# Window attention into a swish feed-forward layer: head-pair loads, coarser crossbar DMAs, and a refitted DMA model in the planner that orders the instructions

## The chip, the cores and the metric

The kernel runs on one core of a Trainium2 chip. The metric is device microseconds of one execution: a median over runs. "Span" is the time from the first to the last instruction in a profiled run, some 2 us less than the device time. Ratios and their intervals use fast runs alone; four of the medians below include one slow run each, that is, one over 1.5% above the fastest of its kernel.

## The reference

Four batches of 8 heads, 768 tokens, 64 channels. Each query sees the 128 keys up to its own and the first 4 keys ("sinks"). The attention output of 3072 tokens x 512 then passes through a feed-forward layer with 2048 hidden channels.

```python
keep   = is_sink | in_window                      # (768, 768)
a      = softmax(where(keep, q @ k.T / 8, -1e9))
x      = (a @ v).transpose(0, 2, 1, 3).reshape(3072, 512)
h      = x @ w_in                                 # 512 -> 2048
out    = (h * sigmoid(beta * h)) @ w_out          # 2048 -> 512
```

## The kernel before

The work is cut into eight half batches (384 tokens), each with four units (pairs of heads). For a unit, q and k are loaded in float32, cast to bfloat16, transposed, multiplied into scores; ScalarE takes the exponential; TensorE multiplies with v; VectorE normalises; the result is transposed into `xT`, the input of the feed-forward part. In half batches 0 to 2 TensorE does the transposes. From half batch 3 on the DMA does them ("crossbar" transposes, DMA_TRANSPOSE in the trace). SyncE issues all loads, stores and crossbar DMAs, one after the other.

The order is fixed before the kernel runs: while it is built, a planner gives every operation a start and an end by assumed durations, and sorts them. Each engine then gets its list and works through it in that order, waiting in line for what an entry needs:

```python
    def place(self, o, at):                       # the planner's clock
        o.at = at
        if o.dma:
            self.free[o.eng] = at + o.queue       # SyncE is taken for the issue
            self.dma_free = max(self.dma_free, at + 1100) + 1.15 * o.ns
            o.end = self.dma_free + 1000          # landed
        else:
            o.end = self.free[o.eng] = at + o.ns
...
    def emit(self, nc, block, sems):              # what each engine gets
        def run(eng, handle):
            for o in self.ops:                    # in the planned order
                if o.eng != eng:
                    continue
                for s, c in o.waits:
                    handle.wait_ge(sems[s], c)
                ins = o.fn(handle)
```

So the DMA engines are one pipe to the planner: each transfer takes 1.15 times its assumed duration, and lands 1 us later. The durations are formulas such as `524288 / 370` ns for a weight load. A planned landing decides at which place of an engine's list the cast of that load stands.

The two DMA issues that the change makes coarser:

```python
    def XT(hb, i, c):                             # q: three DMAs of 4 blocks, k: one of 12
        n, s0 = "qk"[i], 4 * hb % NT
        cs = [c] if i == 0 else list(range(NK))
        ...
            x16[n][hb % NX][:, cs[0]:cs[0] + len(cs), :, :]...), XNS * len(cs), ... queue=XQ)

    def XO(u):                                    # one DMA per unit (3 blocks)
        ...
            xT[:, hp, t0:t0 + HALF]...,
            onorm[on][:, :, :, :]...), XNS * 0.75, ... queue=XQ)
```

and the list of loads, by pairs in half batch 0 only:

```python
    def xl(hb):
        if hb >= XB:                              # XB = 3
            return [(hb, n, i) for n in "qkv" for i in range(NK)]
        if hb:                                    # 1 and 2: q and k whole, 768 KB each
            return [(hb, "q", None), (hb, "k", None)] + [(hb, "v", c) for c in range(NK)]
        return [(0, n, i) for i in range(4) for n in "qk"] + [(0, "v", c) for c in range(NK)]
```

The softmax here doesn't subtract the row's maximum and nothing guards it: scores larger than these inputs give would overflow.

## Time and profile before

| | kernel before |
|---|---|
| time, median of 3 runs | 235.44 us (235.38 to 237.55) |
| profiled span, mean granted clock | 232.9 us, 0.999 |
| first feed-forward matmul | 23.6 us |
| crossbar DMAs, their issue time on SyncE | 40, 59.7 us |
| the planner's own end | 231.4 us |

The table of stretches, SyncE's queue and the chain are shown in the prediction. One more line of before is wanted for later. It is the group of value matmuls (probabilities times v), with TensorE's idle time ahead of them in the last column:

```profile
L708 PE MATMUL P<-vaug,E 128*128 128x65 bf16 x352 | 19.0, 193 | 1.1 <-DVE vaug L453 0.7
```

TensorE waits 1.1 us in all for these 352 matmuls: the order gets to each of them when its inputs are ready.

### The profile page before, as it was taken

The page shows a single profiled execution, that of the slowest core. Times are in us where ns is not written, and L with a number is a line of the kernel's source. Part 1 is how long each engine was busy: PE and PEld are TensorE (multiplying, and loading weights), DVE is VectorE, ACT ScalarE, POOL GpSimd, SP SyncE. Part 2 cuts the span into 40 slices and gives each one's busy share as a digit, 9 for nine tenths or more (in the row PEclk, how much of TensorE's full clock was granted, in tenths as well). Part 3 has the DMA queues.
Part 4 walks back from the last instruction along what each step waited for, and adds up shares of the span by engine and source line. Part 5 has one row for each costly group of instructions (what it writes and reads, how often), then busy time and mean ns, then how long its engine had stood idle before and what let it go on. Part 6 is the DMA issues. An engine that isn't in the chain of part 4 may idle for free.

```text
span 232.9 us, 4577 instructions
## 1 busy us (share of the span) xinstructions
PE 218.9 (94%) x1756; PEld 122.0 (52%) x1756; DVE 136.8 (59%) x291; ACT 152.6 (66%) x276; POOL 72.5 (31%) x163
## 2 busy tenths in 40 slices
PE   7976999899999999998989999999999999999993
PEld 5554555456555555545446555554555555555541
DVE  3795689977764459527739657946553533633310
ACT  3958978578864889439974757776754655645431
POOL 6584943023450337108355104601740000000000
PEclk9999999999999999999999999999999999999999
DMA  6999999999669998694969999977412111011112
GB/s 182 244 335 245 331 363 389 352 235 228 145 155 237 241 272 162 144 176 72 182 133 232 147 227 222 174 170 169 155 34 65 45 45 45 4 45 45 45 48 90
DMA packets 94677, 39.76 MB, mean 171 GB/s; under 512 B 81328, under 2 KB 87488, under 8 KB 94656
## 3 DMA queue, kind: packets, MB, share of 16 engines
q1 hardware_dynamic: 94656, 39.47, 71.4%
q8 instruction: 14, 0.23, 0.4%
q14 instruction: 7, 0.06, 0.1%
HBM read 27.27 MB, written 6.29 MB: 144 GB/s over the span
## 4 chain that ended last, share of the span: by engine, by line
PE 69%; DMA 9%; DVE 8%; ACT 7%; SPq 4%; issue 1%; POOL 0%
PE P L775 34%; PE P L755 26%; DMA v_stage<-in_v_dram 5%; DMA wst<-in_moe_w_in_dram 4%; DVE g L762 3%; ACT E L645 3%; PE P L708 3%; PE P L637 3%; ACT t L760 2%; SPq L740 2%; SPq L512 2%; DVE vaug L453 2%; DVE onorm L714 1%; ACT qkT L448 1%; PE P L698 1%
## 5 line engine op out<-in xcount | busy, mean ns | idle before, releaser
L760 ACT ACTIVATE t<-P,hbeta 128x384 f32<-128x384 f32 x128 | 73.5, 591 | 43.4 <-PE P L755 39.7
L755 PE MATMUL P<-xT,w_in 128*128 128x384 bf16 x512 | 97.3, 326 | 0.9 <-DVE w_in L453 0.6
L775 PE MATMUL P<-w_out,g 128*128 128x512 bf16 x384 | 96.0, 379 | 2.1 <-DVE g L762 1.9
L762 DVE SCALAR_TENSOR_TENSOR g<-t,P 128x384 bf16<-128x384 f32 x128 | 69.2, 548 | 48.4 <-ACT t L760 46.4
L651 POOL TENSOR_SCALAR_AFFINE_SELECT E<-E 128x512 bf16<-128x512 bf16 (+1 forms) x112 | 54.7, 519 | 68.5 <-ACT E L645 67.9
L755 PEld LDWEIGHTS P<-xT,w_in 128*128 128x128 bf16 x512 | 48.0, 98 | 39.3 <-DVE w_in L453 1.4
L775 PEld LDWEIGHTS P<-w_out,g 128*128 128x128 bf16 x384 | 35.9, 98 | 38.3 <-DVE g L762 4.0
L645 ACT ACTIVATE E<-P 128x768 bf16<-128x768 f32 x64 | 45.5, 777 | 5.6 <-PE P L637 5.5
L448 ACT ACTIVATE osb<-P 128x512 f32<-128x512 f32 x19 | 11.4, 598 | 14.6 <-PE P L775 14.6
L708 PE MATMUL P<-vaug,E 128*128 128x65 bf16 x352 | 19.0, 193 | 1.1 <-DVE vaug L453 0.7
L708 PEld LDWEIGHTS P<-vaug,E 128*128 128x128 bf16 x352 | 16.5, 97 | 4.4 <-DVE vaug L453 0.9
L714 DVE TENSOR_TENSOR onorm<-P,rden 128x384 bf16<-128x384 f32 x32 | 17.7, 554 | 0.9 <-DMA xT<-onorm 0.2
L637 PE MATMUL P<-qkT 64*128 64x128 bf16 (+1 forms) x256 | 16.8, 239 | 1.5 <-ACT E L645 1.3
L453 DVE CAST q<-q_stage 128x512 bf16<-128x512 f32 (+1 forms) x19 | 10.1, 541 | 8.5 <-DMA q_stage<-in_q_dram 8.3
L637 PEld LDWEIGHTS P<-qkT 64*128 64x128 bf16 x256 | 8.7, 94 | 11.6 <-issue 4.5
L453 DVE CAST vaug<-v_stage 128x512 bf16<-128x512 f32 x19 | 9.0, 473 | 7.2 <-DMA v_stage<-in_v_dram 7.1
L698 PE MATMUL P<-vS,ES 128*128 128x130 bf16 x64 | 12.7, 220 | 0.0
L712 DVE RECIPROCAL rden<-P 128x6 f32<-128x6 f32 x32 | 6.1, 189 | 9.8 <-PE P L708 9.7
L672 ACT ACTIVATE ES<-P 128x128 bf16<-128x128 f32 (+1 forms) x32 | 11.1, 421 | 0.0
L448 ACT ACTIVATE xT<-P 128x384 bf16<-128x384 bf16 x11 | 5.4, 493 | 7.2 <-PE P L727 7.2
L453 DVE CAST k<-k_stage 128x512 bf16<-128x512 f32 (+1 forms) x15 | 6.9, 465 | 4.9 <-DMA k_stage<-in_k_dram 4.7
L954 PE MATMUL P<-ones 128*128 128x256 bf16 x47 | 8.5, 315 | 1.1 <-POOL ones L459 1.1
(50 smaller groups left out, 101.9 us busy)
## 6 DMA issues: line engine op xcount, KB each, us to landing
v_stage<-in_v_dram SPq DMA_DIRECT2D x24, 256.0 KB, 4.6
out_dram<-osb SPq DMA_DIRECT2D x24, 256.0 KB, 2.4
k_stage<-in_k_dram SPq DMA_DIRECT2D x15, 256.0 KB, 4.6
q_stage<-in_q_dram SPq DMA_DIRECT2D x15, 256.0 KB, 4.8
wst<-in_moe_w_in_dram SPq DMA_DIRECT2D x5, 512.0 KB, 8.6
wst<-in_moe_w_out_dram SPq DMA_DIRECT2D x4, 512.0 KB, 6.8
g<-in_moe_w_out_dram SPq DMA_DIRECT2D x4, 512.0 KB, 7.2
q_stage<-in_q_dram SPq DMA_DIRECT2D x2, 768.0 KB, 7.6
```

Of the source, the lines that this page charges most:

```text
L448: return lambda e: e.activation(dst, src, AF.Copy, bias=0.0, scale=scale)
L453: return lambda e: e.tensor_copy(dst, src)
L637: add("pe", lambda e, dst=dst, own=own, kc=kc, rows=rows, q0=q0, nq=nq: e.matmul(dst, tokens(own, 1, rows, kc, 1)[:, 0, :], tokens(u, 0, r ...
L645: add("act", lambda e, src=src, dst_=dst_: e.activation(dst_, src, AF.Exp, bias=0.0, scale=SCALE), act_ns(256 * n), w=[(k_, z, j) for k_ i ...
L651: add("gp", lambda e, d=d, sg=sg, at_=at_: e.affine_select(d, d, [[0, 2 * len(at_)], [sg, 128]], ALU.is_ge, 0.0, base=min(sg, 0), channel_ ...
L698: add("pe", lambda e, m=m, c0=c0: e.matmul(A[:, c0:c0 + 2 * (D + 1)], ES[z][:, m * 128:(m + 1) * 128], vS[b % 2][:, 2 * hp:2 * hp + 2, :]. ...
L708: e.matmul(A[:, c0:c0 + D + 1], E[z][:, i, hh, :], vaug[vz][:, kb % NK, 2 * hp + hh, :], start=a, stop=o, skip_group_check=True), 39,
L714: add("dve", lambda e: e.tensor_tensor(onorm[on][:, :, :, :].rearrange("p m h d -> p (m h) d"), av[:, :, 0:D], rden[on][:, :].unsqueeze(2) ...
L755: add("pe", lambda e, c=c: e.matmul(hp, w_in16[:, c, m * 128:(m + 1) * 128], xT[:, c, t0:t0 + HALF], start=(c == 0), stop=(c == 3)), mm_ns ...
L760: add("act", lambda e: e.activation(tt[ti][:, :], hp, AF.Tanh, bias=0.0, scale=hbeta[:, m:m + 1]), act_ns(HALF) + 93, r=["hbeta"], w=[("t" ...
L762: add("dve", lambda e: e.scalar_tensor_tensor(gt[T_ % NG][:, m, :], tt[ti][:, :], 1.0, hp, ALU.add, ALU.mult), dve_ns(HALF), r=[("t", ti)] ...
L775: add("pe", lambda e, m=m: e.matmul(P[:, bk, :], gt[T_ % NG][:, m, t * 128:(t + 1) * 128], w_out16[:, m, :], start=(m == 0), stop=(m == NM ...
```

## The change

It has three parts. q and k of half batch 1 are loaded by head pairs, eight DMAs of 192 KB in place of two of 768 KB, so that casts can begin earlier. The crossbar DMAs become fewer: one per tensor and half batch for q and k (q's three of 4 blocks become one of 12, as k has it already), and one per two units for the output. Third, the planner's DMA durations are set to rounded values near the spacings seen in traces, and the factor 1.15 on them goes. Line numbers fall by one to five; L453 of before is L452 of after.

```diff
-            self.dma_free = max(self.dma_free, at + 1100) + 1.15 * o.ns
+            self.dma_free = max(self.dma_free, at + 1100) + o.ns
@@ loads (v, and q and k from half batch 3 on)
-            ... [i], 262144 / 240
+            ... [i], 1110
@@ loads by pairs, whole loads
-            keys, ns = ([i], 196608 / 350) if i is not None else (range(4), 786432 / 350)
+            keys, ns = ([i], 680) if i is not None else (range(4), 2450)
@@ weights; stores
-        ... 524288 / 370, ...
+        ... 1390, ...
-            ... 262144 / 300, ...
+            ... 700, ...
@@ crossbar of q and k
-    def XT(hb, i, c):
-        cs = [c] if i == 0 else list(range(NK))
-            ... XNS * len(cs), ... queue=XQ)        # 700 each block row, 1300
+    def XT(hb, i):
+        cs = list(range(NK))
+            ... 1700, ... queue=1540)
@@ crossbar of the output
-            xT[:, hp, t0:t0 + HALF]..., onorm[on][...]..., XNS * 0.75, ... queue=XQ)
+            xT[:, u // 4, hp:hp + 2, :]..., onorm[:, on:on + 2, :, :]..., 1000, ... queue=1350)
@@ which half batches are loaded and cast by pairs
+    XB, PB = 3, 2
-        if hb:
+        if hb >= PB:
             return [(hb, "q", None), (hb, "k", None)] + [(hb, "v", c) for c in range(NK)]
-        return [(0, n, i) for i in range(4) for n in "qk"] + [(0, "v", c) for c in range(NK)]
+        return [(hb, n, i) for i in range(4) for n in "qk"] + [(hb, "v", c) for c in range(NK)]
```

(Cut: the layouts of `xT` and `onorm` that the wider output transpose needs, and the counts of casts that gate each step.)

More of the change, by code (lines that the diff above doesn't have):

```diff
@@ L348, in _program @@
     NSTG, NX, NV, NT, NE, NON, NG, NTT, NOS, NKS, NWS = 2, 2, 3, 8, 4, 4, 3, 3, 3, 4, 6
-    XB = 3
-    XQ, XNS = 1300, 700
+    XB, PB = 3, 2
     NK = NB // 2
@@ L359, in _program @@
     headm = sb("headm", (128, 2), BF16)
-    xT = sb("xT", (128, 4, NTOK), BF16)
+    xT = sb("xT", (128, NSB, 4, HALF), BF16)
     w_in16 = sb("w_in16", (128, 4, DF), BF16)
@@ L372, in _program @@
     vS = sb("vS", (128, H, D + 1), BF16, 2)
-    onorm = sb("onorm", (128, NK, 2, D), BF16, NON)
+    onorm = sb("onorm", (128, NON, NK * 2, D), BF16)
     rden = sb("rden", (128, 2 * NK), F32, NON)
@@ L502, in load @@
             src = v[b, :, t0 + i * 128:t0 + (i + 1) * 128, :].rearrange("h p d -> p h d")
-            dst, keys, ns = stg[n][z][:, i, :, :], [i], 262144 / 240
+            dst, keys, ns = stg[n][z][:, i, :, :], [i], 1110
         elif hb >= XB:
             src = {"q": q, "k": k}[n][b, :, t0 + i * 128:t0 + (i + 1) * 128, :].rearrange("h p d -> p h d")
-            dst, keys, ns = blocks(stg[n][z])[:, i, :, :], [i], 262144 / 240
+            dst, keys, ns = blocks(stg[n][z])[:, i, :, :], [i], 1110
         else:
@@ L521, in load_w @@
             src = w_out_src[:, 2 * (j - 8):2 * (j - 8) + 2, :]
-        add("sp", lambda e: e.dma_start(wst[j % NWS], src), 524288 / 370, w=[("wst", j % NWS)], dma=f"dw{j % NWS}")
+        add("sp", lambda e: e.dma_start(wst[j % NWS], src), 1390, w=[("wst", j % NWS)], dma=f"dw{j % NWS}")
     def cast_w(j):
@@ L538, in cast @@
             r, w = [("stg", n, z, i), ("vones", hb % NV)], [("v", hb % NV, i)]
-        elif hb == 0:
+        elif hb < PB:
             hs = slice(2 * i, 2 * i + 2)
@@ L549, in cast @@
             r, w = [("stg", n, z, j) for j in range(4)], [(n + "16", hb % NX, j, i) for j in range(4)]
-        if hb == 0 and n != "v":
+        if hb < PB and n != "v":
             ns = {"act": 413, "dve": 400}
@@ L597, in XT @@
             qkT_all[:, hb % (NT // 4), i, cs[0] * 512:cs[0] * 512 + w].rearrange("p (b t) -> p b t", t=128),
-            x16[n][hb % NX][:, cs[0]:cs[0] + len(cs), :, :].rearrange("p c h d -> p (c h d)")), XNS * len(cs),
+            x16[n][hb % NX][:, cs[0]:cs[0] + len(cs), :, :].rearrange("p c h d -> p (c h d)")), 1700,
             r=[(n + "16", hb % NX, j, c_) for j in range(4) for c_ in cs],
-            w=[("qkT", s0 + j, i, c_) for j in range(4) for c_ in cs], dma=f"dx{n}{c}{hb % 2}", queue=XQ)
+            w=[("qkT", s0 + j, i, c_) for j in range(4) for c_ in cs], dma=f"dx{n}{hb % 2}", queue=1540)
     GROUPS = [[[("s", 0, 0), ("s", 0, 1), ("d", 1, 1)], [("d", 2, 2), ("p", 1, 2)]],
@@ L714, in AV @@
         add("dve", lambda e: e.tensor_tensor(
-            onorm[on][:, :, :, :].rearrange("p m h d -> p (m h) d"), av[:, :, 0:D],
+            onorm[:, on, :, :], av[:, :, 0:D],
             rden[on][:, :].unsqueeze(2).to_broadcast([128, 2 * NK, D]), ALU.mult), dve_ns(HALF),
@@ L727, in OT @@
             add("pe", lambda e, m=m: nc.tensor.transpose(
-                mp[:, m * 128:(m + 1) * 128], onorm[on][:, m, :, :].rearrange("p h d -> p (h d)"), ident[:, :]),
+                mp[:, m * 128:(m + 1) * 128], onorm[:, on, 2 * m:2 * m + 2, :].rearrange("p h d -> p (h d)"), ident[:, :]),
                 mm_ns(128), r=[("on", on), "ident"], x=[("B", bs[0])])
-        t0 = b * S + half * HALF
-        any_of(copies(xT[:, hp, t0:t0 + HALF], mp[:, 0:HALF], {"dve": 407, "act": 370}),
+        any_of(copies(xT[:, u // 4, hp, :], mp[:, 0:HALF], {"dve": 407, "act": 370}),
                w=[("xT", hp, 2 * b + half)], x=[("B", bs[0])])
@@ L736, in XO @@
     def XO(u):
-        b, half, hp = where(u)
-        on = u % NON
-        t0 = b * S + half * HALF
+        hp, on = u % 4, u % NON
         add("sp", lambda e: e.dma_start_transpose(
-            xT[:, hp, t0:t0 + HALF].rearrange("p (m t) -> p m t", t=128),
-            onorm[on][:, :, :, :].rearrange("p m h d -> p (m h d)")), XNS * 0.75,
-            r=[("on", on)], w=[("xT", hp, 2 * b + half)], dma=f"dy{on}", queue=XQ)
+            xT[:, u // 4, hp:hp + 2, :].rearrange("p h (m t) -> p (h m) t", t=128),
+            onorm[:, on:on + 2, :, :].rearrange("p o m d -> p (o m d)")), 1000,
+            r=[("on", on), ("on", on + 1)], w=[("xT", hp, u // 4), ("xT", hp + 1, u // 4)], dma=f"dy{on}", queue=1350)
     hi = [0]
@@ L751, in HQ @@
         bs = take(1)
-        t0 = T_ * HALF
         hp = P[:, bs[0], 0:HALF]
@@ L755, in HQ @@
             add("pe", lambda e, c=c: e.matmul(
-                hp, w_in16[:, c, m * 128:(m + 1) * 128], xT[:, c, t0:t0 + HALF],
+                hp, w_in16[:, c, m * 128:(m + 1) * 128], xT[:, T_, c, :],
                 start=(c == 0), stop=(c == 3)), mm_ns(HALF),
@@ L783, in OQ @@
             give([bk])
-            add("sp", lambda e: e.dma_start(out_t[3 * T_ + t], osb[z][:, :]), 262144 / 300, r=[("osb", z)],
+            add("sp", lambda e: e.dma_start(out_t[3 * T_ + t], osb[z][:, :]), 700, r=[("osb", z)],
                 dma=f"do{z}")
@@ L793, in xl, with n_casts @@
             return [(hb, n, i) for n in "qkv" for i in range(NK)]
-        if hb:
+        if hb >= PB:
             return [(hb, "q", None), (hb, "k", None)] + [(hb, "v", c) for c in range(NK)]
-        return [(0, n, i) for i in range(4) for n in "qk"] + [(0, "v", c) for c in range(NK)]
+        return [(hb, n, i) for i in range(4) for n in "qk"] + [(hb, "v", c) for c in range(NK)]
     LOADS = xl(0) + xl(1) + list(range(16)) + [x for hb in range(2, NSB) for x in xl(hb)]
-    CASTS = xl(0) + [(hb, n, i) for hb in range(1, NSB) for n in "qkv" for i in range(NK)]
+    CASTS = [x for hb in range(PB) for x in xl(hb)]
+    CASTS += [(hb, n, i) for hb in range(PB, NSB) for n in "qkv" for i in range(NK)]
+    def n_casts(hb, more):
+        return 11 * min(hb, PB) + 9 * max(hb - PB, 0) + more
     HS = [(T_, m) for T_ in range(NSB) for m in range(NM)]
     OS = [(T_, t, j) for T_ in range(NSB) for t in range(3) for j in range(4)]
-    n_cast, n_w, n_xt = [0], [0], [4 * XB]
+    n_cast, n_w, n_xt = [0], [0], [2 * XB]
     BACKLOG, AHEAD, MARGIN = 6000, 300, 200
@@ L810, in head @@
                 return None
-            if n_cast[0] < (2 * i + 2 if i < 4 else 8 + 9 * (i // 4)):
+            if n_cast[0] < n_casts(i // 4, 2 * (i % 4) + 2 if i < 4 * PB else 6):
                 return None
@@ L821, in head @@
         elif s == "AV":
-            if i >= NU or i >= done["OT"] + NON or i >= min(done["SC"], done["SS"]) or n_cast[0] < 11 + 9 * (i // 4):
+            if i >= NU or i >= done["OT"] + NON or i >= min(done["SC"], done["SS"]) or n_cast[0] < n_casts(i // 4 + 1, 0):
                 return None
@@ L882, in background @@
                 hb, n, c = CASTS[i]
-                t = G.at([("in", hb, n, None if n != "v" and 0 < hb < XB else c)])
+                t = G.at([("in", hb, n, None if n != "v" and PB <= hb < XB else c)])
                 ok = done["T"] >= 4 * (hb - NX + 1) if n != "v" else done["AV"] >= 4 * (hb - NV + 2)
@@ L888, in background @@
                     moved = True
-            hb, x_ = n_xt[0] // 4, n_xt[0] % 4
-            if XB <= hb < NSB and n_cast[0] > 11 + 9 * (hb - 1) + (x_ if x_ < 3 else 5) and min(done["SC"], done["SS"]) >= 4 * (hb - hb % 2):
-                t = G.at([("qk"[x_ // 3] + "16", hb % NX, 0, x_ if x_ < 3 else 2)])
+            hb, x_ = n_xt[0] // 2, n_xt[0] % 2
+            if XB <= hb < NSB and n_cast[0] >= n_casts(hb, 3 + 3 * x_) and min(done["SC"], done["SS"]) >= 4 * (hb - hb % 2):
+                t = G.at([("qk"[x_] + "16", hb % NX, 0, c_) for c_ in range(NK)])
                 if t <= now + AHEAD:
-                    XT(hb, x_ // 3, x_ % 3)
+                    XT(hb, x_)
                     n_xt[0] += 1
-                    if n_xt[0] % 4 == 0:
+                    if n_xt[0] % 2 == 0:
                         for u in range(4 * hb, 4 * hb + 4):
@@ L902, in background @@
             if 4 * XB <= done["OT"] < done["AV"]:
-                t = G.at([("onu", done["OT"])])
-                if t <= now + AHEAD:
+                t = G.at([("onu", done["OT"] + 1)]) if done["OT"] + 1 < done["AV"] else None
+                if t is not None and t <= now + AHEAD:
                     XO(done["OT"])
-                    done["OT"] += 1
+                    done["OT"] += 2
                     moved = True
```

## The prediction

> **What bounds the kernel now.** I read the page first, for the share of each engine and the chain that ended last; then the chain in order of time; then a table of stretches that I cut where the chain changes character; and last the timelines of SyncE (which issues every DMA) and TensorE inside the stretches that lose time.
>
> ```profile
> span 232.9 us, 4577 instructions
> PE 218.9 (94%) x1756; PEld 122.0 (52%) x1756; DVE 136.8 (59%) x291; ACT 152.6 (66%) x276; POOL 72.5 (31%) x163
> PE 69%; DMA 9%; DVE 8%; ACT 7%; SPq 4%; issue 1%; POOL 0%
> ```
>
> TensorE looks nearly full, but 94% is not a measure of work. I take each matmul by the distance between back-to-back starts, as the chain shows it: four matmuls of the first product take 0.65 us, four of the second 0.86, eight score matmuls 0.38, four value matmuls 0.12, one sink matmul 0.06, and 24 input transposes 1.34. With the counts of the page: 512 x 0.1625 = 83.2; 384 x 0.215 = 82.6; 256 x 0.0475 = 12.2; 352 x 0.03 = 10.6; 64 x 0.06 = 3.8; 72 and 36 transposes at 0.056 = 6.0; 16 sink-score matmuls of 384 columns at 0.165 and 16 of 128 at 0.056 = 3.5. Sum 201.9 us. So 31 us of the span are not needed by TensorE's work, and only they can be won, since the change leaves these matmuls as they are (the 47 filler matmuls on a tile of ones are no work). Where the 31 us lie:
>
> ```profile
> core 0: us, PE busy (x) PEld busy (x) DVE busy (x) ACT busy (x) POOL busy (x), PEclk, DMA share, GB/s
> 0.00:4.80 4.80, 3.29 (x16) 2.19 (x16) 1.39 (x2) 1.49 (x2) 3.85 (x21) 1.00 0.54 161
> 4.80:12.40 7.60, 7.08 (x83) 4.59 (x84) 6.12 (x14) 6.30 (x13) 4.15 (x10) 1.00 1.05 253
> 12.40:18.00 5.60, 3.86 (x69) 3.09 (x67) 5.15 (x14) 2.64 (x6) 4.00 (x9) 1.00 1.08 344
> 18.00:23.60 5.60, 3.97 (x47) 2.17 (x44) 2.94 (x5) 5.07 (x9) 3.02 (x4) 1.00 1.00 231
> 23.60:45.00 21.40, 19.44 (x174) 11.45 (x175) 17.89 (x37) 16.96 (x32) 9.57 (x17) 1.00 1.03 363
> 45.00:98.00 53.00, 52.90 (x437) 29.37 (x435) 35.52 (x77) 40.61 (x74) 18.81 (x41) 1.00 0.96 205
> 98.00:124.00 26.00, 23.24 (x236) 12.82 (x234) 14.04 (x33) 18.03 (x35) 12.08 (x26) 1.00 0.81 151
> 124.00:180.00 56.00, 55.85 (x452) 31.13 (x449) 35.02 (x79) 37.06 (x68) 17.06 (x38) 1.00 0.80 159
> 180.00:229.10 49.10, 49.10 (x260) 25.19 (x258) 18.78 (x34) 23.90 (x41) 0.00 (x0) 1.00 0.12 44
> ```
>
> The reader is to compare the length of a stretch with its real matmuls. Up to 23.6 us, when the first feed-forward matmul starts, the attention of half batch 0 and the transposes and scores of half batch 1 amount to 8.7 us: 14.9 are lost, 4.8 of them before any data is there. Counting every distance that exceeds the usual one of its form, I find 3.6 us lost from 23.6 to 45, 2.3 from 45 to 98, 5.7 from 98 to 124, 2.3 from 124 to 180, and nothing after 180: there TensorE works off a backlog without a gap, so a microsecond recovered anywhere before is a microsecond off the end. The last 3.6 us are the output's eviction and store.
>
> Two stretches carry the loss that the change aims at. The first is SyncE's queue from the half batch 1 loads on:
>
> ```profile
> 8.73 0.98 SPq L512 DMA_DIRECT2D q_stage<-in_q_dram  x1
> 9.75 1.11 SPq L512 DMA_DIRECT2D k_stage<-in_k_dram  x1
> ...
> 13.39 7.33 SPq L512 DMA_DIRECT2D v_stage<-in_v_dram  x3
> ```
>
> The k load of 768 KB, issued at 9.75, holds back all casts of k until 18.0, because each cast takes one token block of all eight heads. The DMA engines are full meanwhile (share 1.05 to 1.08). The second is the middle, where SyncE issues without a pause for 26 us:
>
> ```profile
> 98.03 2.77 SPq L596 DMA_TRANSPOSE qkT<-k  x1
> 100.85 4.99 SPq L596 DMA_TRANSPOSE qkT<-q  x3
> 105.88 3.86 SPq L740 DMA_TRANSPOSE xT<-onorm  x3
> 109.79 2.10 SPq L512 DMA_DIRECT2D v_stage<-in_v_dram  x3
> 111.93 6.41 SPq L740 DMA_TRANSPOSE xT<-onorm  x4
> 118.38 2.09 SPq L512 DMA_DIRECT2D k_stage<-in_k_dram  x3
> 120.51 3.26 SPq L512 DMA_DIRECT2D q_stage<-in_q_dram  x3
> 123.81 1.61 SPq L784 DMA_DIRECT2D out_dram<-osb  x1
> ```
>
> The chain runs through it: three output transposes of 1.26 us each on SyncE from 105.88, then the v load of half batch 5 (3.42 us), its cast, and TensorE resumes at 115.44.
>
> **What the Trainium skill says.** "Perfetto Trace Analysis", Identifying the Most-Contended Engine, calls matmul busy time a poor measure; the trace agrees (94% busy, 202 of 232.9 us of work). The same page, What "DMA-bound" means, lists the issuing sequencer as a bound of its own, visible as a solid track of DMA issues; from 98 to 124 us the trace shows just that, with the DMA engines at 0.81. "DMA: Bandwidth & Descriptors", Issuing engines are not separate DMA queues, calls the issue time usually small beside the DMA; here it is not, 1.26 us of the 2.5 us that a four-block transpose takes to land. The same page, Latency and other measured facts, gives DMA transposes 261 to 400 GB/s; the 12-block k transpose at 90.03 landed 3.7 us after its start against 2.5 for a third of its bytes, so the extra 262 KB took 1.2 us, 218 GB/s. Larger transposes cost little more, if nothing else runs.
>
> **The change part by part.**
> Loads by pairs for half batch 1. Two loads of 768 KB become eight of 192 KB, in the form that half batch 0 has. Bytes and runs of contiguous bytes stay; issue is 8 x 0.47 us = 3.8 in place of 2.1, hidden behind full DMA engines. In half batch 0 such loads land about 0.7 us apart. After the third v load lands at about 12.1, pairs would land every 1.4 us or so, the first at about 13.5, the last near 18 as now. Casts become eight of 128x384 (0.42 us on VectorE, 0.5 on ScalarE) in place of six of 128x512, and none may go to GpSimd: about 1 us more for the two engines. So three of the four pairs' transposes, scores and exponentials move from 18-24 us into 13.5-18, where TensorE now runs fillers or waits. The first feed-forward matmul can then start when the first quarter of w_in is cast: that cast ended at 21.7 (20.99 + 0.69), not at 23.6. Gain 1.9 us. Also the exponentials of half batch 1 (8 x 0.70 = 5.6 us of ScalarE) leave the stretch from 21.6 to 28, where ScalarE is full. I give this 1 of the 3.6 us lost up to 45; the rest waits for weights that the DMA delivers at 363 GB/s, which is not changed. Sum 2.9.
> One crossbar DMA per tensor and half batch. Per half batch 3 to 7, the three q transposes (21.6 us on SyncE in all, summed from its timeline) become five of the k form, median 2.01: 10. It saves 11.6 us of SyncE, but q's first block now waits for its last cast.
> Output crossbars per two units. 20 issues, 28.9 us in all, become 10; with an estimate of 1.4 us each, between the 1.26 of a short one and the 2.01 of a long one, 14 us. Saved: 14.9. The first unit of a pair waits for the second, but a feed-forward group needs all four units anyway.
> Together 26.5 us of SyncE between 61 and 178 us, where these issues lie. In 98-124, the k and q issues of one half batch drop from 7.8 us to 4 and seven output issues from 10.3 to 5 (3.5 x 1.4): nine of 26 us come free, and the v load that held TensorE until 115.4 can go several microseconds sooner. Of the 5.7 us lost there I give back 3; the rest is the burst of exponentials ahead of tanhs on ScalarE. Of the 4.6 lost on either side, 0.5.
> The planner's model. It does not run on the chip; it sets the order. Weight loads were planned at 1417 x 1.15 = 1630 ns and land some 1.35 to 1.5 us apart; the new 1390 is nearer. The v load's 1110 also fits the 1.1 us spacing of half batch 0. I count nothing for it, but it makes planned waits more like real ones.
> Sum 2.9 + 3 + 0.5 = 6.4 us; I take off 0.4 for the dearer casts. 235.4 - 6.0 = 229.4.
>
> **The rivals.**
> The loss only moves: the first matmuls then wait for v of half batch 1 (landed near 24) and for weights, because the DMA engines are full to 50 us. For it speaks the DMA share above 1; against it that 1.9 us separate the cast of the weights from their use. If it holds, the head gives under 1 us and the time is 231.5 to 232.
> The new order brings a new stall: a queue planned on an optimistic DMA model waits in line for a load that is late, or long transposes hold back stores and loads behind them (the DMA share was 1.25 from 124 to 132, where transposes and loads met). For it speaks VectorE in the head, where the pair casts are to go: it is busy 5.15 of 5.6 us from 12.4 to 18. It would make 233 to 238.
> Better than I say: the middle loses all its 5.7 us, the head 5, because SyncE and ScalarE both were only late. Then 225 to 226.
>
> **Range and chances.** 229.4 is 2.6% under 235.4; the 2% line is 230.7, so a fifth of the expected gain may fail before the verdict turns. Since the ordering is replanned everywhere, I take 225 to 234.5 for 8 in 10. Faster 0.62, within 2% 0.34, slower 0.04.
>
> **What would show it.** Right: first feed-forward matmul near 21.7 us; fewer fillers; 20 transposes with SyncE idle at times between 98 and 124; real work per stretch still 202 us in all, and no gap in the last 49 us. Wrong: the first feed-forward matmul at 23 us or later (head step); SyncE with gaps there while TensorE still idles 2.8 us (then ScalarE or the order was the cause, not the queue); a long gap before a value matmul or a store.

## The result, and the profile after

| | before | after |
|---|---|---|
| time, median | 235.47 us (235.38 to 237.55, 4 runs) | 242.55 us (241.38 to 243.64, 4 runs) |
| ratio of fast runs, 95% interval | | 1.0278 (1.0204 to 1.0352) |
| profiled span, mean granted clock | 232.9 us, 0.999 | 241.6 us, 0.977 |
| first feed-forward matmul | 23.6 us | 23.0 us |
| crossbar DMAs, issue time | 40, 59.7 us | 20, 36.4 us |
| the planner's own end | 231.4 us | 230.5 us |

The last row isn't from the profile: it is what the planner believed when it made the order. A ratio is the mean time of one kernel's fast runs over that of the other's fast runs of the same rounds, so it isn't quite the ratio of the medians quoted. The clock isn't the cause: another run of the kernel after had a granted clock of 1.000 and took 242.6 us.

The page of the kernel after, its first lines and the chain by engine:

```profile
span 241.6 us, 4512 instructions
PE 221.1 (92%) x1728; PEld 123.1 (51%) x1753; DVE 144.2 (60%) x301; ACT 153.4 (63%) x276; POOL 69.0 (29%) x155
PE 65%; SPq 13%; DMA 12%; DVE 4%; POOL 2%; ACT 2%; issue 2%
```

SyncE's queue and the DMA together rose from 13% of the chain to 25%. (PE has 1728 records beside 1753 weight loads: 25 matmul records are missing, so counts are better read from the PEld column.) The table of stretches, cut at the same places as before; columns are PE, PEld, DVE, ACT and POOL busy time with counts, then the granted clock, DMA share and GB/s:

```profile
12.40:18.00 5.60, 4.10 (x72) 2.94 (x72) 5.45 (x15) 3.74 (x9) 4.25 (x11) 1.00 0.99 307
23.60:45.00 21.40, 17.10 (x136) 9.22 (x134) 17.50 (x36) 13.85 (x25) 7.51 (x13) 0.92 1.02 352
45.00:98.00 53.00, 50.34 (x431) 28.38 (x438) 39.35 (x88) 37.36 (x68) 19.97 (x42) 1.00 1.15 233
98.00:124.00 26.00, 22.23 (x177) 11.84 (x179) 16.03 (x36) 17.44 (x33) 7.95 (x17) 0.87 1.12 212
124.00:180.00 56.00, 54.58 (x479) 31.40 (x486) 32.10 (x71) 39.59 (x71) 20.05 (x44) 1.00 0.54 108
```

From 23.6 to 45 TensorE did 134 weight loads where the kernel before did 175, and from 98 to 124 it did 179 in place of 234. Such counts mislead, since by the prediction's distances a first-product matmul takes 0.1625 us and a value matmul 0.03, and 35 of the 55 loads missing from 98 to 124 are those of value matmuls. So here are the weight loads of the feed-forward part alone, counted from the start (first product + second product; `prof LABEL --windows ... --engine PEld` with `--tile w_in` and `--tile w_out`; `after_old_model` is an experiment below):

```text
by us                  45        98       124       180
before               79+8   192+118   232+152   387+252
after                64+8   173+104   220+136   358+232
after_old_model      64+4   183+104   239+152   380+252
```

At 180 us the kernel after is 29 and 20 behind, which at 0.1625 and 0.215 us each is 9.0 us; the spans differ by 8.7. Of it, 2.4 us are lost up to 45 us, 3.7 from 45 to 98 and 3.6 from 124 to 180; from 98 to 124 the attention part falls behind instead. The DMA share from 98 to 124 is 1.12, where it was 0.81. Two stretches are shown more closely, in which the prediction had counted on gains (1 us and 3 us).

In the first of them the chain in order of time (start, length, what) runs through one weight load:

```profile
23.67 9.43 DMA g<-in_moe_w_in_dram
...
33.12 0.69 DVE w_in L452
```

The load landed at 33.10. The one before it had landed at 29.57, 3.53 us earlier, although the weight loads after it came 1.35 us apart. TensorE's first-product matmuls stop for it until the casts are done. How much of the model's cost lies in this stretch stays open: `after_old_model`, which is 7.4 us faster, is as far behind at 45 us (64+4), `after_factor` is 1.3 us less so (77+4).

The second stretch shows how one late load becomes everybody's wait. VectorE's timeline (start, length, line, operation; in brackets the idle time ahead and what ended it):

```profile
107.67 0.43 DVE L452 CAST k<-k_stage 128x512 bf16<-128x512 f32 x1 [2.65 <-DMA k_stage<-in_k_dram]
108.88 0.52 DVE L452 CAST k<-k_stage 128x512 bf16<-128x512 f32 x1 [0.78 <-DMA k_stage<-in_k_dram]
109.32 0.62 DVE L656 TENSOR_TENSOR E<-E,maskS 128x512 bf16<-128x512 bf16 x1
...
112.42 0.47 DVE L452 CAST q<-q_stage 128x512 bf16<-128x512 f32 x1 [1.47 <-DMA q_stage<-in_q_dram]
112.81 0.62 DVE L656 TENSOR_TENSOR E<-E,maskS 128x512 bf16<-128x512 bf16 x1
...
113.57 0.56 DVE L713 TENSOR_TENSOR onorm<-P,rden 128x384 bf16<-128x384 f32 x1
```

and TensorE's over the same time:

```profile
107.16 1.04 PE L770 MATMUL P<-w_out,g 128*128 128x512 bf16 x4
109.99 0.35 PE L707 MATMUL P<-vaug,E 128*128 128x65 bf16 x6 [1.80 <-DVE E L656]
...
114.18 0.51 PE L707 MATMUL P<-vaug,E 128*128 128x65 bf16 x6 [1.56 <-DVE onorm L713]
```

Read the first from above: VectorE sits idle for 2.65 us with its list stopped at the cast of a k load that has not landed. Behind that cast, in the list, stands the masking of E, which TensorE's value matmuls need. So TensorE waits 1.80 us for a 0.62 us operation, which in turn waits for data of a later half batch that TensorE doesn't want yet. The same happens again at 112.42. Over the whole run the idle time ahead of value matmuls rose from 1.1 us to 6.1:

```profile
L707 PE MATMUL P<-vaug,E 128*128 128x65 bf16 x352 | 19.8, 196 | 6.1 <-DVE E L656 1.8
```

Why does the cast stand there? The planner believed that the load would be there. Laying the planner's own times beside the trace gives, for the last DMA that was planned to land by a given time, how late it landed (us, negative is early):

```text
planned landing by       25    50    80   100   120   140    plan's end   measured span
before                 -0.2  -1.6  -0.6  -0.6   2.8   2.7       231.4         232.9
after                   3.3   4.8   7.2   9.3  12.2  11.7       230.5         241.6
```

The k load above was planned to land at 98.41, and landed at 107.64. In the kernel before no load was over 3.6 us late (a store was, by 5.1). The kernel after falls behind from the head on and never gets back.

How far off is the model? In the kernel after, the 19 loads from the last k pair of half batch 1 to the last weight were planned to land over 25.6 us (17.13 to 42.70). They took 28.3 (19.68 to 47.98), 1.11 times as long. Between the planned landings of 55.37 and 99.52 us the real ones took 48.5 in place of 44.15, 1.10 times. The single durations are not bad: pairs land 0.57 us apart (planned 0.68), weights 1.35 (planned 1.39); only the 256 KB blocks of q and k are clearly short, 1.2 us apart at the median between 60 and 109 us (planned 1.11). But the fourth pair load came 3.00 us after the third (14.38 to 17.38), and one weight 3.53 after another. From 60 to 109 us three such gaps, each about 1.1 us longer than planned, make 3.3 of the 4.3 us lost on the plan. The old formulas with 1.15 planned 29.85 us for those 19 loads, where the kernel before took 27.5: pessimistic by 9%.

### The profile page after: what moved, and what is told of

Same layout as the page of the kernel before. It is cut to its first block, busy times and chain, and to the rows that moved or that the text cites.

```text
span 241.6 us, 4512 instructions
## 1 busy us (share of the span) xinstructions
PE 221.1 (92%) x1728; PEld 123.1 (51%) x1753; DVE 144.2 (60%) x301; ACT 153.4 (63%) x276; POOL 69.0 (29%) x155
## 4 chain that ended last, share of the span: by engine, by line
PE 65%; SPq 13%; DMA 12%; DVE 4%; POOL 2%; ACT 2%; issue 2%
PE P L770 29%; PE P L750 28%; SPq L511 10%; DMA q_stage<-in_q_dram 5%; DMA g<-in_moe_w_in_dram 4%; PE P L707 3%; PE P L636 3%; POOL E L650 2%; DMA qkT<-q 2%; SPq L521 2%; DMA v_stage<-in_v_dram 1%; DVE g L757 1%; ACT t L755 1%; PE P L697 1%; PE P L667 1%
## 5 line engine op out<-in xcount | busy, mean ns | idle before, releaser
L757 DVE SCALAR_TENSOR_TENSOR g<-t,P 128x384 bf16<-128x384 f32 x128 | 70.0, 551 | 56.3 <-ACT t L755 53.8
L750 PE MATMUL P<-xT,w_in 128*128 128x384 bf16 x512 | 100.3, 331 | 1.5 <-DVE w_in L452 1.0
L770 PE MATMUL P<-w_out,g 128*128 128x512 bf16 x359 | 92.7, 381 | 2.4 <-DVE g L757 1.0
L650 POOL TENSOR_SCALAR_AFFINE_SELECT E<-E 128x512 bf16<-128x512 bf16 (+1 forms) x112 | 57.1, 541 | 58.7 <-ACT E L644 58.2
L707 PE MATMUL P<-vaug,E 128*128 128x65 bf16 x352 | 19.8, 196 | 6.1 <-DVE E L656 1.8
L707 PEld LDWEIGHTS P<-vaug,E 128*128 128x128 bf16 x352 | 16.8, 99 | 11.0 <-DVE E L656 2.3
L447 ACT ACTIVATE osb<-P 128x512 f32<-128x512 f32 x21 | 12.6, 598 | 11.3 <-PE P L770 11.2
L713 DVE TENSOR_TENSOR onorm<-P,rden 128x384 bf16<-128x384 f32 x32 | 17.8, 557 | 1.0
L452 DVE CAST q<-q_stage 128x512 bf16<-128x512 f32 (+1 forms) x20 | 11.4, 569 | 9.7 <-DMA q_stage<-in_q_dram 9.5
L452 DVE CAST k<-k_stage 128x512 bf16<-128x512 f32 (+1 forms) x19 | 9.5, 506 | 7.1 <-DMA k_stage<-in_k_dram 6.7
L452 DVE CAST vaug<-v_stage 128x512 bf16<-128x512 f32 x19 | 9.3, 490 | 4.0 <-DMA v_stage<-in_v_dram 3.6
L656 DVE TENSOR_TENSOR E<-E,maskS 128x512 bf16<-128x512 bf16 x15 | 7.3, 484 | 4.2 <-ACT E L644 4.0
L447 ACT ACTIVATE xT<-P 128x384 bf16<-128x384 bf16 x8 | 3.9, 488 | 8.0 <-PE P L726 8.0
```

The costliest lines, as they stand in the source:

```text
L447: return lambda e: e.activation(dst, src, AF.Copy, bias=0.0, scale=scale)
L452: return lambda e: e.tensor_copy(dst, src)
L650: add("gp", lambda e, d=d, sg=sg, at_=at_: e.affine_select(d, d, [[0, 2 * len(at_)], [sg, 128]], ALU.is_ge, 0.0, base=min(sg, 0), channel_ ...
L707: e.matmul(A[:, c0:c0 + D + 1], E[z][:, i, hh, :], vaug[vz][:, kb % NK, 2 * hp + hh, :], start=a, stop=o, skip_group_check=True), 39,
L713: add("dve", lambda e: e.tensor_tensor(onorm[:, on, :, :], av[:, :, 0:D], rden[on][:, :].unsqueeze(2).to_broadcast([128, 2 * NK, D]), ALU. ...
L750: add("pe", lambda e, c=c: e.matmul(hp, w_in16[:, c, m * 128:(m + 1) * 128], xT[:, T_, c, :], start=(c == 0), stop=(c == 3)), mm_ns(HALF), ...
```

## The experiments

**Theory.** The factor 1.15 carried the pauses of the DMA. Without it the plan is about a tenth too fast, lateness adds up, and engines that work strictly in order stop behind casts. **Rivals.** The pairs bring the loss (casts and transposes in the wrong place in the head); or the coarse crossbars do (a longer wait for the last block of each, or a fuller DMA).

### Which part: each undone in after, or done alone on before

The planner's old numbers and factor, all else as after:

```diff
-            self.dma_free = max(self.dma_free, at + 1100) + o.ns
+            self.dma_free = max(self.dma_free, at + 1100) + 1.15 * o.ns
@@ and 1110, 680, 2450, 1390, 700 back to the formulas; XT 2100, queue 1300; XO 1050, queue 1300
```

> The changed kernel with the planner's former DMA model (former durations, times 1.15; a 12-block transpose planned as three former 4-block ones). Theory 'model' (the new model plans DMAs to land too early, so the in-order queues wait for them): the loss is gone, 232 to 237 us, ratio to before 0.985 to 1.005. Theories 'pairs' and 'coarse crossbars' (the new DMAs themselves cost the time): stays at 240 to 243, ratio 1.02 to 1.03.

235.16 us, ratio 0.9962 (0.9934 to 0.9991), span 233.7. The slowdown is gone: the model is its cause. But the gain of 2.6% predicted for the rest hasn't come either.

The new numbers alone, on before (its issues and loads kept; crossbar costs scaled to their sizes):

```diff
-            self.dma_free = max(self.dma_free, at + 1100) + 1.15 * o.ns
+            self.dma_free = max(self.dma_free, at + 1100) + o.ns
@@ and the new durations; XT 567 each block row, XO 500
```

> The kernel before with only the planner's new DMA model. Theory 'model': it alone does the harm, 239 to 243 us, ratio 1.015 to 1.03. Theories 'pairs' and 'coarse crossbars': 233 to 237, ratio 0.99 to 1.005.

251.53 us (250.57 by its fast runs), ratio 1.0711 (1.0615 to 1.0807), far past the 239 to 243 expected. No operation was changed here, only the order; and the planner thought this the best of all, with an end at 229.5. Measured span 248.0, and loads planned for 140 us land 20.2 us late. VectorE's timeline shows the same stop as in after:

```profile
109.75 0.43 DVE L452 CAST vaug<-v_stage 128x512 bf16<-128x512 f32 x1 [3.38 <-DMA v_stage<-in_v_dram]
```

After without the pairs:

```diff
-    XB, PB = 3, 2
+    XB, PB = 3, 1
```

> The changed kernel with half batch 1 loaded and cast as before (two loads of 768 KB, casts by token block). Theory 'model': still slow, 239 to 243 us, ratio 1.015 to 1.03. Theory 'pairs' (the head is where it is lost): 234 to 237, ratio 0.995 to 1.005.

241.28 us, ratio 1.0247 (1.0192 to 1.0301). Under the new model the pairs make little difference; they are not what makes after slow. (By the 2% line this run is unclear, but its interval lies wholly above 1.)

The pairs alone, on before (old model, fine crossbars):

```diff
-    XB = 3
+    XB, PB = 3, 2
@@ and the list of loads, casts and their counts as in after
```

> The kernel before with only the first loads by head pairs. Theory 'model', and my prediction's step for the head: 232 to 235.5 us, ratio 0.985 to 1.0, the first feed-forward matmul near 21.7 us. Theory 'pairs': 239 to 243, ratio 1.015 to 1.03.

241.89 us, ratio 1.0273 (1.0205 to 1.0341): a loss where the prediction had a gain, and inside the range that I had given to the theory "pairs". The first feed-forward matmul moved to 22.4 us, but the end moved out. By the same count of feed-forward weight loads it is about 2.3 us behind the kernel before at 45 us (65+8), and 7.3 at 180 (358+240), so most of the loss comes after the head. ScalarE's timeline and then TensorE's, near 110 us:

```profile
109.94 0.63 ACT L447 ACTIVATE q<-q_stage 128x512 bf16<-128x512 f32 x1 [3.38 <-DMA q_stage<-in_q_dram]
```

```profile
111.80 1.46 PE L750 MATMUL P<-xT,w_in 128*128 128x384 bf16 x4 [2.88 <-ACT E L644]
```

Again a cast that stands too early in an engine's list, this time on ScalarE with an exponential behind it. So a stop of this kind is possible under the old model too: loads planned for 120 us land 5.5 us late here. SyncE is busy for 25.0 of the 26 us from 98 to 124 with the fine crossbars. That this leaves it no room to catch up is my reading, and no run tests it: in the kernel before SyncE is as busy (25.1).

### The coarse crossbars alone

Both, old model, no pairs:

```diff
-    XB, PB = 3, 2
+    XB, PB = 3, 1
@@ and the old model as in after_old_model
```

> Both coarser crossbars, the planner's former DMA model, half batch 1 loaded as before. Theory 'model, and the coarse crossbars help the middle' (after_old_model lost some 2 us between 98 and 124 us where the kernel before lost 5.7): 229 to 232.5 us, ratio 0.975 to 0.99, which would beat both kernels. Rival 'coarse crossbars are neutral': 234 to 237.

232.8 us, ratio 0.9853 (0.9827 to 0.988), just above the range expected. SyncE now has gaps, such as the 4.1 us between these two rows (its timeline, start and length):

```profile
102.26 3.56 SPq L511 DMA_DIRECT2D v_stage<-in_v_dram  x3
109.96 1.22 SPq L736 DMA_TRANSPOSE xT<-onorm  x1
```

and TensorE does 50+39 feed-forward weight loads from 98 to 124 us, where before did 40+34 and after 47+32: 2.7 us more work than before by the prediction's distances, where 3 were predicted. The whole stretch:

```profile
98.00:124.00 26.00, 24.81 (x244) 14.35 (x242) 14.33 (x36) 19.46 (x37) 13.28 (x27) 1.00 0.96 193
```

The q and k crossbars alone, and the output crossbars alone, each on before:

```diff
@@ before_coarse_xt: XT of after at 2100, queue 1300; XO of before
@@ before_coarse_xo: XO of after at 1050, queue 1300; XT of before
```

> The kernel before with one crossbar DMA per tensor and half batch alone (former model). 'Coarse crossbars help the middle': 232 to 235, ratio 0.985 to 1.0, about half of the gain. 'Neutral': 235 to 236.5. 'The longer DMA harms': 238 and more.

232.91 us, ratio 0.9842 (0.9802 to 0.9883).

> The kernel before with output crossbars per two units alone (former model). 'Help the middle': 232 to 235, ratio 0.985 to 1.0. 'Neutral': 235 to 236.5. 'The pair waits for its second unit and harms': 238 and more.

232.25 us, ratio 0.9828 (0.9801 to 0.9856): the lowest median of a correct kernel, though its interval overlaps those of the other two. Either part alone gives what both give. That the stretch has only so much to recover is a guess; the profile of `before_coarse_xt`, taken in its slowest run (235.13 us), shows hardly more feed-forward work from 98 to 124 (38+38 weight loads) than the kernel before (40+34). The coarse crossbars are not a cause of the slowdown.

### Which piece of the model: the factor

After, with nothing but the factor put back; the new durations stay:

```diff
-            self.dma_free = max(self.dma_free, at + 1100) + o.ns
+            self.dma_free = max(self.dma_free, at + 1100) + 1.15 * o.ns
```

> The changed kernel with only the factor 1.15 on DMA time put back; the new durations stay. If the missing margin is what hurts: 233 to 237 us, ratio 0.985 to 1.005. If the new durations by themselves plan a bad order: 239 to 243.

234.94 us, ratio 0.9933 (0.9907 to 0.996). One number, 3.5% (1.0278 / 0.9933). Loads planned for 140 us are 0.6 us late, and the plan's end of 232.9 stands beside a span of 233.8. With the factor the new durations are harmless.

The waits of the casts show the mechanism (`prof LABEL --waits --window 45:180`): VectorE and ScalarE wait 17.8 us in all for loads to land in the kernel after, and for none in `after_factor` or `after_old_model`. Yet the loads themselves come no sooner there. Of the 50 loads of half batches 2 to 7, 46 landed earlier in the kernel after than in `after_factor`, by up to 18.8 us; the k load of 107.64 us landed at 117.6 in the faster kernel, planned for 117.2. So what differs is the place of the cast in its engine's list, and not how early the load lands. Nor is the sum of such waits the price: in the kernel before it is 14.6 us, with only 1.1 us of idle time ahead of value matmuls, and in `coarse_old_model` none. (GpSimd's waits, which occur in all of these runs, are left out.)

Two other values, with `1.07 * o.ns` and `1.30 * o.ns` in the same line:

> The changed kernel with the factor 1.07 on DMA time in the planner. In the changed kernel the DMAs between 50 and 100 us of the plan took about 1.10 times as long as planned. If the rate of the plan is what counts: between the neighbours, 235.5 to 240.5 us, ratio 1.0 to 1.02, DMAs late by about half as much as in the changed kernel (4 to 8 us at 140 us). If only the order happens to be good at 1.15 and 1.30: 241 and more, or under 235.

> The changed kernel with the factor 1.30 on DMA time in the planner, twice the former margin. Theory 'margin': too late costs less than too early, 233 to 239 us, ratio 0.985 to 1.015, whereas its own plan ends at 240.1. Rival 'the best plan is the truest one': 239 and more.

1.07 gave 235.27 us, ratio 0.9938 (0.99 to 0.9975), just under the range expected: I had thought half the margin would buy about half the loss back, but it buys nearly all of it. Loads are still up to 3.9 us late with it. 1.30 gave 236.23 us, ratio 0.999 (0.9962 to 1.0018). So 1.30 costs about 0.6% against 1.15, which is within the scatter of orders found below, and no margin at all costs 3.5%.

Instead of the factor a fixed margin, each load landing 3 us later in the plan:

```diff
-            o.end = self.dma_free + 1000
+            o.end = self.dma_free + 4000
```

> The changed kernel with one constant of the planner changed: it takes each DMA to land 3 us later for those who wait for it (4000 ns in place of 1000 after its turn), while the DMA durations, and so the moments at which loads are issued, keep the new model. Theory 'late landings block in-order queues' (a cast that waits for a late load holds up the masks and normalisations queued behind it on VectorE, and these hold up TensorE): 233 to 238 us, ratio 0.985 to 1.01. Rival 'too many DMAs are issued too early and crowd each other': stays at 239 to 244.

243.93 us, ratio 1.0329 (1.0285 to 1.0372). The theory in this form fell: it isn't that a load needs a few microseconds of slack. The comparison of plan and trace shows why. Loads are 0.8 us late at 60 us, 3.8 at 90, 7.7 at 120: the 3 us are used up by 60 us, and the lateness goes on growing to 120 us, since the rate is wrong. A proportional margin works here and 3 us do not; a larger fixed one wasn't tried. The time lies in the range of the rival, that DMAs issued too early crowd each other. The traces speak against it: in the kernel after the loads land earlier than in `after_factor`, as said, and a crossbar of q or k takes 4.3 us from issue to landing at the median, against 4.2 there. No run fully separates the moments of issue from the planned landings.

Is any new order good for such a change? Two neutral replans, with the planner's cost of a hand-over between engines at 190 ns:

```diff
-    HOP = 180
+    HOP = 190
```

> The changed kernel with a neutral change of the planner (180 ns to 190 ns per hop between engines), which moves the order about. Theory 'new model without margin': still slow, 238 to 248 us, ratio over 1.01. Rival 'one unlucky order': 232 to 237.

> coarse_old_model with a neutral change of the planner (190 ns in place of 180 per hop). If the coarse crossbars are what helps: 231.5 to 234.5 us, ratio 0.978 to 0.993. If coarse_old_model was a lucky order: 235 and more.

After so replanned: 240.88 us, ratio 1.02 (1.0163 to 1.0236); the slowdown stays. `coarse_old_model` so replanned: 234.13 us, ratio 0.9882 (0.9815 to 0.9949); the gain stays. A meaningless change of order moves the time by 0.3 to 0.8% (0.9853 to 0.9882, 1.0278 to 1.02), so smaller differences between these kernels carry no meaning. Over all correct kernels: the five orders planned with the factor 1.00 took 240.88 to 251.53 us, and the ten experiments with 1.07 or more 232.25 to 236.23, but for one, `before_pairs` (241.89).

### Is it the bytes, or the order? (wrong results on purpose)

The same order as after, but each weight load brings half of its bytes. The plan is untouched, as the assumed durations are kept; the result is wrong.

```diff
-            src = w_in_src[:, 2 * h:2 * h + 2, m * 512:(m + 1) * 512]
+            src = w_in_src[:, 2 * h:2 * h + 1, m * 512:(m + 1) * 512]
@@ w_out the same; the cast reads the half twice
```

> Wrong result on purpose: each weight load moves half of its bytes (one of its two row blocks, which the cast then reads twice); plan and order are those of the changed kernel. If lateness of the real DMAs against the plan is what costs, the head's part of it goes (TensorE was some 5 us behind its plan at 50 us): 234 to 238 us, less than 242.5 by 4 to 8. If the order itself is bad whatever the DMAs do: 240 to 243.

238.41 us, ratio 1.008 (1.0042 to 1.0118): over 4 of the 6.5 us are back, though it is just above the range expected. Then half the bytes of q, k and v too, from half batch 2 on:

```diff
-            src = v[b, :, t0 + i * 128:t0 + (i + 1) * 128, :]...
+            hl = H if hb < PB else H // 2
+            src = v[b, 0:hl, t0 + i * 128:t0 + (i + 1) * 128, :]...
@@ q and k the same
```

> Wrong result on purpose: the changed kernel, plan and order untouched, with half of the bytes in each weight load and in each q, k and v load of half batches 2 to 7. If the order is good and only the DMAs' lateness against the plan costs: TensorE stays within 3 us of its plan, span 230 to 233.5, 231 to 235 us. If the order is bad in itself or the crossbars set the pace: 237 and more.

232.29 us, ratio 0.9827 (0.9785 to 0.9869). The span is 229.9 us, with a plan of 230.5. The order of the kernel after is a good one, if its loads come when it says. At 180 us TensorE has done 398+256 feed-forward weight loads, in place of 358+232, and from 45 to 180 us no cast of VectorE or ScalarE waits for a load. From 23.6 to 45 us it does 160 weight loads of all kinds in place of 134:

```profile
23.60:45.00 21.40, 17.67 (x160) 9.90 (x160) 19.89 (x40) 13.56 (x25) 9.44 (x15) 1.00 0.86 234
```

This settles the cause: instruction for instruction the same order, 10 us apart in the medians, by nothing but the bytes that the DMAs move. Lighter loads in themselves bring little where the plan has its margin: halved weights alone took off 0.8 and 1.6 us below. The halving of q, k and v was not run on such a kernel.

### What the pairs cost

Under the old model, after without pairs is at 0.9853 and with them at 0.9962: pairs cost 1.1%, about 2.6 us. TensorE's timeline of `after_old_model` in the head:

```profile
29.32 0.50 PE L750 MATMUL P<-xT,w_in 128*128 128x384 bf16 x2 [1.54 <-DVE w_in L452]
31.08 4.00 PE L750 MATMUL P<-xT,w_in 128*128 128x384 bf16 x14 [1.26 <-DVE w_in L452]
```

Here the feed-forward part did begin at 21.6 us, and then TensorE waited 1.54 and 1.26 us for weights, which come no sooner. If weights are the whole of it, halving their bytes must remove the cost. Both kernels, with the light weights of above:

> Wrong result on purpose: both coarse crossbars, loads by pairs, former DMA model, and weight loads of half the bytes. If pairs lost their gain because TensorE then waits for w_in (waits of 1.5 and 1.3 us near 30 us): these waits vanish and it runs 2 us or more faster than after_old_model, 230.5 to 233 us, level with or faster than coarse_light. If pairs cost by their casts or their smaller DMAs: still 2 us or more slower than coarse_light.

> Wrong result on purpose: both coarse crossbars, half batch 1 loaded as before, former DMA model, and weight loads of half the bytes. Without pairs TensorE waits little for weights (0.6 us in the kernel before), so little is won: 231 to 233 us, within 1.5 us of coarse_old_model. If it falls by 3 us or more, weights held this order too.

With pairs 233.61 us, ratio 0.9894 (0.9869 to 0.9918), outside both guesses; without 231.99 us, ratio 0.9822 (0.9778 to 0.9866). The light weights take off 1.6 us with pairs and 0.8 without, so of 2.4 us between the medians 0.8 was weight supply, and 1.6 remain. In the lighter kernel the first wait falls to 0.32 us, but the second stays at 1.26: its weights had landed by 25.8 us, and their cast stood in VectorE's list until 29.30, behind the cast before it, a normalisation and a feed-forward product. That's order again, and not supply. How much of it comes from pairs as such, and how much from the scatter of replanning, stays open.

The same question with the new durations and the factor 1.15, so `after_factor` without pairs:

```diff
-    XB, PB = 3, 2
+    XB, PB = 3, 1
```

> The changed kernel with half batch 1 loaded as before and with the factor 1.15 put back on the new durations: both coarse crossbars, a model with margin, no pairs. If margin and coarse crossbars are what counts: 230 to 234 us, ratio 0.975 to 0.99, as coarse_old_model. If the new durations hurt beside the lacking margin: 235 and more.

233.59 us, ratio 0.9867 (0.9828 to 0.9905), against 0.9933 with pairs: 0.7%, no more than a neutral replan moved. So pairs cost between 0.3% (1.0247 to 1.0278) and 2.7%, depending on what they are put into, and bring a gain nowhere. The smaller of these costs are within the scatter of replanning.

## Why the prediction was wrong

| step of the prediction | predicted | measured |
|---|---|---|
| pairs, less dearer casts | -2.5 us | +2.6 us (0.9853 to 0.9962, old model) |
| coarse crossbars | -3.5 us | -3.5 us (ratio 0.9853 of 236.2) |
| the planner's model | 0 | +7.5 us (0.9962 to 1.0278) |
| sum | -6.0 us | +6.6 us |

The measured column is a chain of ratios from before to after, so its sum agrees with the measured 6.5 by construction; a neutral replan moves a row by up to 1.9 us (0.8%), and the sizes depend on the order in which the parts are put in (pairs alone on before: +6.4 us; model alone on before: +16.8).

**The planner's model** is the step that failed: "I count nothing for it, but it makes planned waits more like real ones." It does the reverse, and costs 7.5 us where nothing was counted; the factor alone makes 3.5%. I compared the new durations with single spacings in the trace, 1.35 to 1.5 us between weight loads and 1.1 for v, and found them nearer than the old. That comparison was right and beside the point. The factor 1.15 did not correct the durations; it stood for the pauses between them. With the factor the plan gave 19 loads in the head 9% more time than they took, without it 10% less. The two errors are about the same size and not of the same price. A load that is early waits in its buffer. A load that is late stops an in-order list, and all that stands behind it.

**The second rival** named this mechanism word for word, "a queue planned on an optimistic DMA model waits in line for a load that is late", and gave it 233 to 238 us. What was mis-sized is the accumulation: I thought of one stop, but the lateness grows with each load (3.3 us at 25, 12.2 at 120), as the error is in a rate. I looked for support of it in VectorE's load in the head, and so missed the diff's plainest line. The trace of before held the answer: by the new durations those 19 loads sum to 25.6 us, and they had landed over 27.5.

**The head.** The matmul did move to 21.6 us under the old model, as predicted (21.7), and the gain was not kept, which is the first rival: TensorE then waits at 29 and 31 us for weights. In after itself it stands at 23.0, the prediction's own sign of a failed head step. The sign itself tells little: that matmul starts at 28.8 us in `after_factor` and at 25.2 in `before_coarse_xo`, both faster than after.

**The crossbars** were right in mechanism, since SyncE comes free and TensorE does more work in the middle. The size agrees to the tenth, and this closely it is luck: orders scatter by 0.8%, and the parts, 14.9 and 11.6 us of issue time, don't add. Saved issue time on SyncE: 26.5 us predicted, 30.2 in `coarse_old_model` and 23.3 in after. At the median an output pair takes 1.27 or 1.35 us (estimated 1.4); a transpose of 12 blocks takes 1.47 in `coarse_old_model`, and 1.52 (q) or 1.85 (k) in after (estimated 2.0). In after the gain can't be seen: from 83 to 124 us SyncE's timeline has no gap over 0.6 us. Part of that is waiting inside a crossbar's own time (2.8 of 3.5 us at 91.55), and the 21 loads take 0.9 us each on average to issue. The k load planned at 93.53 us came at 104.03, in line behind them.

**The bound** was read correctly in that recovered time ahead of 180 us shows at the end one for one; lost time does so too. The trace's "long gap before a value matmul", which the prediction listed as a sign of being wrong, is there (1.80 us at 109.99).

**Open:** why single loads come 3.00 or 3.53 us after their forerunners; the part of the pairs' cost that light weights did not remove; and the scatter of neutral replans, of which I have two.

## What to carry to other kernels

When the order of a kernel comes from a plan, compare the plan's sum over a stretch with the trace, not its single durations: the plan with the earliest end here (229.5 us) took longest (248.0). Keep a proportional margin on transfers, since too much cost 0.6% at most and none cost 3.5%, and try placing casts of prefetched data behind work that is wanted now (not tested here). Change such a model in a step of its own, so that it can't hide what the other parts gain.

## What the Trainium skill lacked or had wrong

- "DMA: Bandwidth & Descriptors", Latency and other measured facts: it gives the HBM access latency as 0.2 us on average and 2 us at high load, but has nothing on gaps between loads of one queue. Here pair loads landed 0.57 us apart except for one gap of 3.00 us, and weight loads 1.35 except for one of 3.53; over 19 loads the sum was 1.11 times the planned one. Whether that latency causes the gaps, no run here shows.
- "DMA: Bandwidth & Descriptors", Issuing engines are not separate DMA queues: the issue time is called usually small beside the DMA. For crossbar DMAs it wasn't: 40 of them took 59.7 us of SyncE's 232.9, mostly about 1.26 us each beside a median of 2.6 or 2.7 to landing, and halving their number gained 1.5% (ratio 0.9853).
- "Perfetto Trace Analysis", DMA Optimizations: splitting DMAs may let the whole finish sooner if the DMA engines are generally idle. The page isn't wrong; here its condition didn't hold: with a DMA share of 1.05 to 1.08 in the head, splitting two loads into eight gained nothing (0.9853 without, 0.9962 with). That the full DMA engines are the reason, no run shows.
- I found no page on how much margin an order fixed at build time needs for its loads: here factors of 1.00, 1.07, 1.15 and 1.30 gave 242.55, 235.27, 234.94 and 236.23 us.
